# Four-layer attention kernel: weights' maxima from ScalarE magnitudes, half-precision parts on ScalarE, one chunk's queries moved into the first tail

## The chip, the cores and the metric

The kernel runs on one core of a Trainium2 chip. Its engines each have an instruction queue of their own that is served in order: TensorE (PE in the profile; its weight loads are PEld), VectorE (DVE), ScalarE (ACT), GpSimd (POOL) and SyncE (SP), which issues the transfers. The metric is the device time of one execution in microseconds, as the median of several runs. Before the change it is 2862.91 us (three runs, 2860.83 to 2866.21).

## The reference

Four layers, A, B, A, B, each adds its attention to the stream x (2048 tokens of 512). A is attention over a sliding window of 256 tokens, B over all tokens; both have 32 heads of 16. A layer normalises its input over the features, without weights.

```python
x = A_x
x = x + _A_ref(_layernorm(x, axis=-1), A_wqkv, A_wo)
x = x + _B_ref(_layernorm(x, axis=-1), B_wqkv, B_wo)
x = x + _A_ref(_layernorm(x, axis=-1), A_wqkv, A_wo)
x = x + _B_ref(_layernorm(x, axis=-1), B_wqkv, B_wo)

# both: q, k, v = x @ wqkv, split into 32 heads of 16
scores = jnp.einsum("bhqd,bhkd->bhqk", q, k) * (Dh ** -0.5)
scores = jnp.where(mask[None, None], scores, -1e9)   # A only: 0 <= i - j < 256
p = _softmax(scores, axis=-1)
o = jnp.einsum("bhqk,bhkd->bhqd", p, v)
return o.transpose(0, 2, 1, 3).reshape(B, S, D) @ wo
```

B_x is an input that nothing reads.

## The kernel before

**Tiling.** Tokens go in four chunks of 512 (NQ, index c), heads in four tiles of eight (NHT, index t) and eight quads of four (qd). A number that must be nearly of float32 precision is held as two float16 parts, a high part and the rest, and a projection takes three products of parts (TERMS). Twelve products of 128x128 by 512 (four slices of the features by three terms) make one tile of a projection, and four tiles one work of 48 products: K (keys), Q (queries), VV (values), OO (output projection with the next layer's normalisation).

**Preparing the weights.** Both layer types have four matrices: s = 0 queries, 1 keys, 2 values, 3 output. Each is scaled by a power of two per output column before it is split. `maxima` (line 277) finds the largest magnitude of each column: two VectorE reductions over the four slices, then transposes on TensorE and one more reduction. `scales` (line 305) makes powers of two and spreads them with a TensorE product. `parts` (line 327) multiplies by the scale, casts to the high part, subtracts for the low part and stores both (`wd`). Three matrices of A are prepared at the start by other functions (`first_maxima`, and `parts` with `act` true: VectorE multiplies, ScalarE casts). The other five go through `prep` (line 343) during layer 0, where GpSimd does all of `parts`: (0, 3) and (1, 1) in chunk 0, (1, 0) and (1, 2) in chunk 1, (1, 3) in chunk 2.

**Normalising.** `norm` (line 431) turns four tiles of tokens into `xn` (float32), its float16 high part `xh[:, 0]` and the rest `xh[:, 1]`, all on VectorE. A transposing transfer on SP's queue (T, line 461) then makes `xc`, from which K, Q and VV work.

**Attention.** Scores (line 663) go to PSUM, ScalarE takes their exponential `e` (line 667), in windowed layers GpSimd masks the edges of `e` (lines 729 and 732), and TensorE multiplies with the values (line 739 windowed, 707 full), two tiles of scores later. In layers 0 and 2 this alternates on TensorE with one tile of a work at a time. In layers 1 and 3 (`PH["full"]`) a work's products are cut into four strips of 32 columns (line 408) and spread over the steps.

**Order.** TensorE's order is that in which the program is written out: `attention` (line 897) runs the attention steps and draws works from lists (`side0` to `side3`, lines 1039 to 1071) by a clock of its own. A generator that yields a wait is taken up again when that clock has passed it. A tail, `tails[l]` (line 1075), holds the works between two layers; in it the first work that is ready goes first. `Side` with its due cost (line 808) spreads the works over the steps. The other engines' order, and the order of transfers on SP, come from the framework's scheduler. Two buffers hold weights (WB), four hold raw and prepared weights (tag `vf`).

Of the kernel before, what the change touches and what calls it, by code (L numbers as in the profile page):

```python
# [19 lines left out]
P = 128  # L20
# [168 lines left out]
def fast_path(ctx, tc, flag, a_x, a_wqkv, a_wo, b_wqkv, b_wo, out):  # L189
# [87 lines left out]
    def maxima(ty, s, raw):  # L277

        n = f"{ty}_{s}"
        if s == 3:  # L280
            for k in range(NC):
                nc.vector.tensor_scalar(raw[:, k, :], raw[:, k, :], upv[:, ty, k:k + 1], None, op0=ALU.mult)
        cm = CM[ty, s] = vp.tile([P, NHT], F32, name=f"wc{n}", tag="wc", bufs=8)
        am = vp.tile([P, D], F32, name=f"wa{n}", tag="dn", bufs=2)
        for h in range(2):
            f = slice(h * D // 2, (h + 1) * D // 2)
            nc.vector.tensor_reduce(am[:, f], raw[:, :, f].rearrange("p k f -> p f k"), axis=AX.X, op=ALU.max,
                                    apply_absolute_value=True)
            yield
        pt = bank().rearrange("p (t f) -> p t f", f=P)  # L290
        for t in range(NHT):
            nc.tensor.transpose(pt[:, t, :], am[:, t * P:(t + 1) * P], ident)
        nc.vector.tensor_reduce(cm, pt, axis=AX.X, op=ALU.max)
# [33 lines left out]
    def parts(ty, s, raw, act):  # L327

        dnb = DN.pop((ty, s))
        w = wp.tile([P, NC, 2, D], F16, name=f"w{ty}_{s}", tag="vf", bufs=NQ)  # L330
        for k in range(NC):
            r = raw[:, k, :]
            (nc.vector if act else nc.gpsimd).tensor_tensor(r, r, dnb, ALU.mult)
            if act:
                nc.scalar.activation(w[:, k, 0, :], r, AF.Copy)
            else:
                nc.gpsimd.tensor_copy(w[:, k, 0, :], r)
            nc.gpsimd.tensor_tensor(w[:, k, 1, :], r, w[:, k, 0, :], ALU.subtract)  # L338
            yield
        nc.sync.dma_start(wd[ty, s], w)  # L340
        WT[ty, s] = w

    def prep(ty, s):
        raw = load_w(ty, s)
        yield wait(14)
        for _ in maxima(ty, s, raw):
            yield wait(4)
        yield -spent(1.0)
        for _ in scales(ty, s):
            yield wait(4)  # L350
        if (ty, s) == (1, 0):
            share(1)
        yield -spent(0.5)
        for _ in parts(ty, s, raw, False):
            yield wait(2.5)
        WT.pop((ty, s))

# [73 lines left out]
    def norm(l, c, xs):  # L431

        mv = ST.pop((l, c))[1]
        y = rsqrt(nc, vp, f"{l}_{c}", mv[:, :, 1])
        out = []
        for i in range(4):
            xn = vp.tile([P, D], F32, name=f"xn{l}_{c}_{i}", tag="xn", bufs=1)
            xh = vp.tile([P, 2, D], F16, name=f"xh{l}_{c}_{i}", tag="xh", bufs=XNB)
            norm1 = lambda o: nc.vector.tensor_scalar(o, xs[i], mv[:, i, 0:1], y[:, i:i + 1], op0=ALU.subtract, op1=ALU.mult)  # L439
            norm1(xn)  # L440
            norm1(xh[:, 0])
            nc.vector.tensor_tensor(xh[:, 1], xn, xh[:, 0], ALU.subtract)  # L442
            out.append(xh)
# [587 lines left out]
    def F(*parts):  # L1031

        def gen():
            for p in parts:
                fill(*p)
                yield wait(8)
# [20 lines left out]
    def side1():  # L1057
        a = [Q(1, c, False) for c in (1, 2, 3)]
        for c in range(3):
# [3 lines left out]
    def side3(t, c):  # L1063
# [5 lines left out]
        if (t, c) != (0, 0):  # L1069
# [4 lines left out]
             [side3(t, c) for t in range(NHT) for c in range(NQ)]]  # L1074
    tails = {0: [OO(0, 3), VV(1, 2), T(1, 3), K(1, 3)],
             2: [OO(2, 3), VV(3, 1), VV(3, 2), Q3(0, 0, True), T(3, 3), K3(3, 0, True)]}
# [49 lines left out]
```

## Time and profile before

The profiled execution took 2864.46 us; its span, from the first to the last instruction, is 2862.7 us.

| | before |
|---|---|
| median of three runs | 2862.91 us |
| lowest, highest | 2860.83, 2866.21 us |
| profiled execution, its span | 2864.46 us, 2862.7 us |
| busy in the span: PE, ACT, DVE, POOL | 2668.1 (93%), 2352.5 (82%), 1048.1 (37%), 627.5 (22%) us |
| mean granted TensorE clock | 0.979 |
| transfers | 363.10 MB, 127 GB/s |

How to read it: the page cuts the span into 40 equal slices and gives the busy share of each in tenths. A table by windows has one row a stretch, with start and end in us, its length, busy us of each engine with the number of instructions in brackets, the granted clock as a share of full speed, the transfers' share and GB/s. A list of waits has who waited on which line, for whom, and total us, number and longest. A group has line, engine, operation, output and inputs by the program's names, shapes and count; then busy us, mean ns of one; then the idle time before them and what ended it. A timeline row has start, duration, engine, line and operation; the bracket at its end is the engine's idle time before it and what ended that. SPq is SP issuing transfers. The clock of a stage and its waits are read together.

### The profile page before, as it was taken

The page shows a single profiled execution, that of the slowest core. Times are in us where ns is not written, and L with a number is a line of the kernel's source. Part 1 is how long each engine was busy: PE and PEld are TensorE (multiplying, and loading weights), DVE is VectorE, ACT ScalarE, POOL GpSimd, SP SyncE. Part 2 cuts the span into 40 slices and gives each one's busy share as a digit, 9 for nine tenths or more (in the row PEclk, how much of TensorE's full clock was granted, in tenths as well). Part 3 has the DMA queues.
Part 4 walks back from the last instruction along what each step waited for, and adds up shares of the span by engine and source line. Part 5 has one row for each costly group of instructions (what it writes and reads, how often), then busy time and mean ns, then how long its engine had stood idle before and what let it go on. Part 6 is the DMA issues. An engine that isn't in the chain of part 4 may idle for free.

```text
span 2862.7 us, 58733 instructions
## 1 busy us (share of the span) xinstructions
PE 2668.1 (93%) x23298; PEld 766.6 (27%) x23298; DVE 1048.1 (37%) x2194; ACT 2352.5 (82%) x2643; POOL 627.5 (22%) x1183
## 2 busy tenths in 40 slices
PE   8777989799999999999999888999999999999997
PEld 4222433322222222222223333322222222222221
DVE  7667656411113212311224667722222322223222
ACT  3443656299999999999996666569999999999996
POOL 3547565101100000000003567500000000000000
PEclk9888999899999999999999999999999999999998
DMA  6857666522223222322343665542433333333331
GB/s 225 229 181 191 219 189 201 179 101 88 88 70 104 90 70 88 111 83 70 97 112 116 177 189 146 161 135 89 126 102 103 113 121 119 111 101 110 112 97 57
DMA packets 317423, 363.10 MB, mean 127 GB/s; under 512 B 120913, under 2 KB 223825, under 8 KB 309841
## 3 DMA queue, kind: packets, MB, share of 16 engines
q1 hardware_dynamic: 317136, 359.24, 41.5%
q8 instruction: 185, 3.03, 0.4%
q14 instruction: 102, 0.83, 0.1%
HBM read 229.64 MB, written 96.99 MB: 114 GB/s over the span
## 4 chain that ended last, share of the span: by engine, by line
PE 68%; ACT 10%; DVE 8%; issue 6%; DMA 3%; POOL 3%; SPq 1%; ACTq 0%; DVEq 0%; POOLq 0%
PE acc L707 28%; PE s L663 18%; ACT e L667 9%; PE b L411 9%; PE acc L408 8%; PE acc L739 3%; PE bs L411 2%; DVE ot L633 1%; DMA oh<-hl 1%; DVE xh L442 1%; SPq L650 1%; POOL w L338 1%; POOL e L732 1%; DVE xn L439 1%; DVE xh L439 1%
## 5 line engine op out<-in xcount | busy, mean ns | idle before, releaser
L667 ACT ACTIVATE e<-s 128x1024 f32<-128x1024 f32 (+2 forms) x2432 | 2235.3, 1199 | 115.1 <-PE s L663 108.1
L707 PE MATMUL acc<-e,vt 128*17 128x512 f32 x8192 | 1078.0, 598 | 3.7 <-DVE ot L633 1.5
L663 PE MATMUL s<-qt,kt 64*128 64x512 f16 (+3 forms) x5504 | 791.1, 355 | 70.8 <-ACT e L667 36.3
L663 PEld LDWEIGHTS <-kt 64*128 64x128 f16 x5504 | 222.6, 94 | 894.6 <-issue 851.3
L646 POOL TENSOR_TENSOR hl<-o,hl 128x512 f16<-128x512 f32 x64 | 74.2, 1159 | 999.8 <-DVE hl L645 923.3
L633 DVE STREAM_TRANSPOSE ot<-acc 128x512 f32<-128x512 f32 x128 | 91.2, 712 | 545.6 <-PE acc L707 448.0
L732 POOL TENSOR_SCALAR_AFFINE_SELECT e<-e 128x256 f32<-128x256 f32 x512 | 229.6, 456 | 160.1 <-ACT e L667 159.7
L739 PE MATMUL acc<-e,vt 128*17 128x384 f32 (+2 forms) x2816 | 213.4, 398 | 27.5 <-POOL e L729 26.6
L729 POOL TENSOR_SCALAR_AFFINE_SELECT e<-e 128x256 f32<-128x256 f32 x448 | 205.3, 464 | 113.7 <-ACT e L667 111.8
L707 PEld LDWEIGHTS acc<-e,vt 128*17 128x17 f32 x8192 | 136.3, 95 | 343.6 <-issue 314.5
L411 PE MATMUL b<-xc,w 128*128 128x512 f16 x636 | 154.6, 396 | 7.3 <-DMA xc<-xh 6.2
L492 DVE TENSOR_SCALAR sp<-acc,es 128x512 f16<-128x512 f32 x32 | 23.9, 748 | 323.6 <-PE acc L408 323.6
L490 ACT ACTIVATE sp<-b,es 128x512 f16<-128x512 f32 x53 | 36.4, 687 | 123.4 <-PE b L411 119.5
L498 POOL TENSOR_TENSOR sq_h<-sp_h 128x512 bf16<-128x512 f16 x27 | 29.1, 1077 | 451.5 <-DVE sp_h L492 451.5
L408 PE MATMUL acc<-xc,w 128*32 128x512 f16 x1536 | 127.2, 379 | 0.4 <-DVE sp L493 0.2
L498 POOL TENSOR_TENSOR sq<-sp 128x512 bf16<-128x512 f16 x32 | 33.3, 1039 | 405.3 <-DVE sp L492 405.3
L411 PE MATMUL b<-wv,xc 128*128 128x512 f16 x456 | 110.1, 395 | 11.0 <-DMA wv<-wd 11.0
L408 PE MATMUL acc<-xc,w_h 128*32 128x512 f16 x1296 | 114.5, 379 | 2.3 <-DVE km L530 2.3
L586 ACT ACTIVATE vt<-b 128x512 f32<-128x512 f32 x38 | 22.7, 597 | 102.7 <-PE b L411 102.7
L621 DVE TENSOR_TENSOR dx<-acc,gcol 128x512 f32<-128x512 f32 x60 | 41.5, 691 | 178.8 <-PE acc L408 178.8
L408 PE MATMUL acc<-wo,oh 128*32 128x512 f16 x1296 | 102.8, 379 | 0.7 <-DVE m L542 0.7
L411 PE MATMUL b<-wo,oh 128*128 128x512 f16 x390 | 91.5, 384 | 9.7 <-DMA oh<-hl 9.0
(164 smaller groups left out, 1728.0 us busy)
## 6 DMA issues: line engine op xcount, KB each, us to landing
kt<-kf SPq DMA_DIRECT2D x128, 512.0 KB
qt<-qs SPq DMA_DIRECT2D x128, 256.0 KB
xd<-x SPq DMA_DIRECT2D x96, 256.0 KB
x<-xd SPq DMA_DIRECT2D x96, 256.0 KB
w<-wd SPq DMA_DIRECT2D x22, 1024.0 KB
kt<-kw SPq DMA_DIRECT2D x64, 256.0 KB
oh<-hl SPq DMA_DIRECT2D x512, 32.0 KB
wv<-wd SPq DMA_DIRECT2D x15, 1024.0 KB
```

The costliest lines, as they stand in the source:

```text
L408: nc.tensor.matmul(ps[g:g + 32], a[:, g:g + 32], b, start=(i == 0), stop=(i == len(pairs) - 1), skip_group_check=True)
L411: nc.tensor.matmul(ps, a, b, start=(i == 0), stop=(i == len(pairs) - 1))
L439: norm1 = lambda o: nc.vector.tensor_scalar(o, xs[i], mv[:, i, 0:1], y[:, i:i + 1], op0=ALU.subtract, op1=ALU.mult)
L498: nc.gpsimd.tensor_tensor(sq, sp[:, 0], sp[:, 0], ALU.mult)
L633: nc.vector.transpose(ot.rearrange("p b r -> p (b r)"), a)
L646: (nc.gpsimd if l % 2 else nc.vector).tensor_tensor(hl[:, 1], o, hl[:, 0], ALU.subtract)
L663: nc.tensor.matmul(ps[:, h, s0:s0 + wd_], kt[R * h:R * h + R, pr, kc:kc + P], qt[R * h:R * h + R, pr, qc:qc + wd_], start=True, stop=True)
L667: nc.scalar.activation(e[:, :, w0:w1], ps[:, :, w0:w1], AF.Exp, scale=SCALE)
L707: nc.tensor.matmul(a[32 * h:32 * h + DH + 1, :], V[l, j // 4][:, j % 4, 4 * qd + h, :], es_[h // 2][:, h % 2, :], start=(j == 0), stop=(j ...
L729: nc.gpsimd.affine_select(v, v, pattern=[[0, 2], [-1, P]], compare_op=ALU.is_gt, fill=0.0, base=0, channel_multiplier=1)
L732: nc.gpsimd.affine_select(v, v, pattern=[[0, 2], [1, P]], compare_op=ALU.is_ge, fill=0.0, base=0, channel_multiplier=-1)
L739: nc.tensor.matmul(a[32 * h:32 * h + DH + 1, q * P:(q + nb) * P], V[l, (4 * c + j) // 4][:, j % 4, 4 * qd + h, :], es_[h // 2][:, h % 2, s ...
```

## The change

`maxima` now takes a prepared-weight tile at once and uses its high half, as bfloat16, for magnitudes that ScalarE writes slice by slice. VectorE takes three maxima of two slices each instead of the two reductions. The scaling of the output weights by `upv` moves from VectorE to ScalarE. `maxima` yields three times instead of two, and `prep` waits 3 instead of 4 at each.

`parts` runs its three steps shifted by one slice each, and the cast is ScalarE's always; GpSimd keeps the multiplication (where `act` is false) and the subtraction.

`norm` has ScalarE write the high part, as y times x plus nb, with nb = -mean times y a new 128x4 VectorE product. For l = 2 VectorE copies it from `xn` instead.

`F`, which writes constant rows of the score operands, waits 15 on the program's clock before its first fill. The queries of layer 1's chunk 1 move from `side1` to the first tail.

```diff
     def maxima(ty, s, raw):
         n = f"{ty}_{s}"
-        if s == 3:
-            for k in range(NC):
-                nc.vector.tensor_scalar(raw[:, k, :], raw[:, k, :], upv[:, ty, k:k + 1], None, op0=ALU.mult)
+        w = WT[ty, s] = wp.tile([P, NC, 2, D], F16, name=f"w{n}", tag="vf", bufs=NQ)
+        ab = w[:, :, 0, :].bitcast(BF16)
+        for k in range(NC):
+            if s == 3:
+                nc.scalar.activation(raw[:, k, :], raw[:, k, :], AF.Copy, scale=upv[:, ty, k:k + 1])
+            nc.scalar.activation(ab[:, k, :], raw[:, k, :], AF.Abs)
+            if k % 2:
+                yield
         cm = CM[ty, s] = vp.tile([P, NHT], F32, name=f"wc{n}", tag="wc", bufs=8)
         am = vp.tile([P, D], F32, name=f"wa{n}", tag="dn", bufs=2)
-        for h in range(2):
-            f = slice(h * D // 2, (h + 1) * D // 2)
-            nc.vector.tensor_reduce(am[:, f], raw[:, :, f].rearrange("p k f -> p f k"), axis=AX.X, op=ALU.max,
-                                    apply_absolute_value=True)
-            yield
+        for k in (0, 2):
+            nc.vector.tensor_tensor(ab[:, k, :], ab[:, k, :], ab[:, k + 1, :], ALU.max)
+        nc.vector.tensor_tensor(am, ab[:, 0, :], ab[:, 2, :], ALU.max)
+        yield
...
     def parts(ty, s, raw, act):
         dnb = DN.pop((ty, s))
-        w = wp.tile([P, NC, 2, D], F16, name=f"w{ty}_{s}", tag="vf", bufs=NQ)
-        for k in range(NC):
-            r = raw[:, k, :]
-            (nc.vector if act else nc.gpsimd).tensor_tensor(r, r, dnb, ALU.mult)
-            if act:
-                nc.scalar.activation(w[:, k, 0, :], r, AF.Copy)
-            else:
-                nc.gpsimd.tensor_copy(w[:, k, 0, :], r)
-            nc.gpsimd.tensor_tensor(w[:, k, 1, :], r, w[:, k, 0, :], ALU.subtract)
+        w = WT.pop((ty, s), None) or wp.tile([P, NC, 2, D], F16, name=f"w{ty}_{s}", tag="vf", bufs=NQ)
+        for k in range(NC + 2):
+            if k < NC:
+                (nc.vector if act else nc.gpsimd).tensor_tensor(raw[:, k, :], raw[:, k, :], dnb, ALU.mult)
+            if 0 < k <= NC:
+                nc.scalar.activation(w[:, k - 1, 0, :], raw[:, k - 1, :], AF.Copy)
+            if k > 1:
+                nc.gpsimd.tensor_tensor(w[:, k - 2, 1, :], raw[:, k - 2, :], w[:, k - 2, 0, :], ALU.subtract)
             yield
         nc.sync.dma_start(wd[ty, s], w)
-        WT[ty, s] = w
...
         for _ in maxima(ty, s, raw):
-            yield wait(4)
+            yield wait(3)
...
+        nb = vp.tile([P, 4], F32, name=f"nb{l}_{c}", tag="lnb")
+        nc.vector.scalar_tensor_tensor(nb, mv[:, :, 0], -1.0, y, op0=ALU.mult, op1=ALU.mult)
         for i in range(4):
...
-            norm1 = lambda o: nc.vector.tensor_scalar(o, xs[i], mv[:, i, 0:1], y[:, i:i + 1], op0=ALU.subtract, op1=ALU.mult)
-            norm1(xn)
-            norm1(xh[:, 0])
+            nc.vector.tensor_scalar(xn, xs[i], mv[:, i, 0:1], y[:, i:i + 1], op0=ALU.subtract, op1=ALU.mult)
+            if l == 2:
+                nc.vector.tensor_copy(xh[:, 0], xn)
+            else:
+                nc.scalar.activation(xh[:, 0], xs[i], AF.Identity, bias=nb[:, i:i + 1], scale=y[:, i:i + 1])
             nc.vector.tensor_tensor(xh[:, 1], xn, xh[:, 0], ALU.subtract)
...
     def F(*parts):
         def gen():
+            yield wait(15)
             for p in parts:
...
     def side1():
-        a = [Q(1, c, False) for c in (1, 2, 3)]
+        a = [Q(1, c, False) for c in (2, 3)]
...
-    tails = {0: [OO(0, 3), VV(1, 2), T(1, 3), K(1, 3)],
+    tails = {0: [OO(0, 3), VV(1, 2), Q(1, 1), T(1, 3), K(1, 3)],
```

On TensorE the order of the works stays as it was up to the first tail. There the moved queries come between the values of chunk 2 and the output projection of chunk 3. The transposes for the maxima and the products that spread the scales come one group later than before.

More of the change, by code (lines that the diff above doesn't have):

```diff
@@ L355, in prep @@
             yield wait(2.5)
-        WT.pop((ty, s))
     def share(ty):
```

## The prediction

> **What bounds the kernel now.** I read the page's 40 slices first. TensorE (PE) is full nearly everywhere but in the first fifth; ScalarE (ACT) is full in the two long plateaus and half empty before and between them.
>
> ```profile
> PE   8777989799999999999999888999999999999997
> ACT  3443656299999999999996666569999999999996
> ```
>
> Then the busy time by stage: layer 0 with its preparation is 0 to 520, its tail 520 to 580, layer 1 580 to 1520.
>
> ```profile
> core 0: us, PE busy (x) PEld busy (x) DVE busy (x) ACT busy (x) POOL busy (x), PEclk, DMA share, GB/s
> 100.00:200.00 100.00, 72.66 (x533) 26.14 (x533) 61.61 (x140) 46.08 (x65) 61.49 (x116) 0.90 0.67 195
> 200.00:300.00 100.00, 76.57 (x580) 29.89 (x580) 71.49 (x122) 40.41 (x49) 62.92 (x110) 0.84 0.67 188
> 520.00:580.00 60.00, 43.46 (x196) 18.51 (x193) 24.84 (x54) 9.45 (x15) 0.00 (x0) 0.86 0.52 167
> 580.00:1520.00 940.00, 928.36 (x8681) 219.81 (x8684) 203.12 (x452) 938.16 (x1018) 69.86 (x65) 1.00 0.29 88
> ```
>
> So layer 1 hangs on ScalarE (938.16 of 940.00). In layer 0 no engine is full, yet TensorE idles a quarter of the time: its order is written by hand, so it stands wherever the next product's input is late. Third, its waits from 0 to 580, as total, count, longest:
>
> ```profile
> PE acc L739 <- POOL e L729: 24.7, 10, 6.3
> PE bs L411 <- DMA xc<-xh: 15.4, 1, 15.4
> PE b L411 <- DMA wv<-wd: 11.0, 2, 8.2
> PE b L515 <- DVE sp L493: 8.4, 1, 8.4
> PE b L411 <- DMA xc<-xh: 6.2, 1, 6.2
> PE b L292 <- DVE km L530: 4.6, 1, 4.6
> ```
>
> The longest total is for GpSimd (POOL): its edge masks stand behind weight products and casts. The next is the gap in the tail, then a weight load late on SP's queue, then VectorE (DVE) twice. The change touches all of these, but only in layer 0 and the tails can it gain.
>
> **The change, part by part.** Groups up to 540 us:
>
> ```profile
> L338 POOL TENSOR_TENSOR w<-wr,w 128x512 f16<-128x512 f32 x32 | 41.6, 1316 | 48.3 <-ACT w L335 48.2
> L287 DVE TENSOR_REDUCE wa<-wr 128x256 f32<-128x1024 f32 x10 | 19.4, 1962 | 0.0
> L442 DVE TENSOR_TENSOR xh<-xn,xh 128x512 f16<-128x512 f32 x24 | 18.1, 753 | 0.1
> L439 DVE TENSOR_SCALAR xh<-x,mv,y 128x512 f16<-128x512 f32 x24 | 14.3, 617 | 0.0
> L337 POOL CAST w<-wr 128x512 f16<-128x512 f32 x20 | 13.6, 692 | 0.0
> L335 ACT ACTIVATE w<-wr 128x512 f16<-128x512 f32 x12 | 7.4, 630 | 11.9 <-DVE wr L333 11.9
> ```
>
> *Casts leave GpSimd.* Five prepared weights have four casts each: 20 x 0.692 = 13.8 us, 8 of them with each of two pairs of weights and 4 with the last. GpSimd's waits at TensorE add up to 24.7, more than 13.8, and come where the masks are queued behind this work, so I take all 13.8 as gain. Bounds: 24.7 if the waits go entirely, and nothing, if the masks are as late as before. On ScalarE the same casts cost 20 x 0.630 = 12.6 us, hidden in its empty half of layer 0 (row 200 to 300: 40.41 of 100); without that cover they would cost 12.6.
>
> *Maxima.* Per weight, two reductions of 1.962 us give way to four ScalarE magnitudes and three VectorE maxima, neither shown before. For a magnitude I take 0.630, the cast's row, between 0.6 and 0.7. For a maximum of two 512-wide rows I take 0.753, the row L442, the dearer end; half of it is the cheap one. The four scalings of each output weight move to ScalarE too and lie in the same cover. TensorE feels all this only at the two waits for VectorE:
>
> ```profile
> 199.38 0.62 PE L515 MATMUL b<-sq,hsum 128*32 128x512 bf16 x4 [8.44 <-DVE sp L493]
> 207.44 1.97 PE L292 MATMUL b<-ident,wa 128*128 128x128 f32 x8 [4.63 <-DVE km L530]
> ```
>
> There four half reductions (7.8 us) and four xh conversions (4 x 0.617 = 2.5) leave VectorE and six maxima (4.5) come: 5.8 less. But the evacuation sp that ends the first wait now starts on ScalarE behind four conversions and four magnitudes (8 x 0.630 = 5.0) that themselves wait for VectorE's statistics. So I take 4.0 of the 13.0; bounds 0 and 13.0.
>
> *Normalised tokens.* xh leaves VectorE in layers 0, 1 and 3's normalisations (layer 2's keeps it as a copy from xn, so ScalarE's plateau is not charged). It pays where the normalisation is waited for, in the tail:
>
> ```profile
> 518.77 2.76 PE L411 MATMUL bs<-wv,xc 128*128 128x512 f16 x12
> 526.55 2.75 PE L411 MATMUL b<-wv,xc 128*128 128x512 f16 x12
> 546.58 1.29 SPq L461 DMA_TRANSPOSE xc<-xh  x1
> 549.13 0.69 DVE L442 TENSOR_TENSOR xh<-xn,xh 128x512 f16<-128x512 f32 x1
> 550.44 0.69 DVE L442 TENSOR_TENSOR xh<-xn,xh 128x512 f16<-128x512 f32 x1
> 555.10 4.62 PE L411 MATMUL bs<-xc,w 128*128 128x512 f16 x12 [15.43 <-DMA xc<-xh]
> ```
>
> The last two tiles take 1.31 each with xh already done; four at that pace after the added 128x4 product instead of twelve operations bring the last xh about 1.2 us forward: -1.2 here, -1.2 in the tail of layer 2. Bounds 0 and 2.5 (four conversions).
>
> *Queries of chunk 1 in the first tail.* 48 products. Three groups of twelve start 7.78 us apart (518.77 to 526.55), 2.59 each: 4 x 2.59 = +10.4 us of a stage where TensorE is the bound. In the changed order they stand ahead of the output projection of chunk 3, and the gap of 15.43 us comes after that projection, so nothing fills it; its evacuations and twelve stores go under the projection. What layer 1 gets back: its first chunk, where these products stood, counted by exponentials (L667) and side products (L408):
>
> ```profile
> 640.00:700.00 60.00, 60.00 (x67) 1.00 0.30 95
> 760.00:820.00 60.00, 60.00 (x67) 1.00 0.26 81
> ```
>
> ```profile
> 640.00:700.00 60.00, 14.47 (x172) 4.87 (x164) 1.00 0.30 95
> 760.00:820.00 60.00, 6.26 (x72) 2.09 (x72) 1.00 0.26 81
> ```
>
> 67 exponentials in 60 us with 172 side products, and 67 with 72: ScalarE sets the pace, so taking products out gives nothing (bounds 0 and 10.4). The other eleven works of the layer need chunk 0's result and cannot move up.
>
> *SP's queue.* The scheduler reorders it. Early, one more transpose stands behind the fourth weight's load; late, the value weights of chunk 2 come ahead of two weight stores and two output moves:
>
> ```profile
> 71.53 8.81 SPq L461 DMA_TRANSPOSE xc<-xh  x2
> 252.63 3.98 PE L411 MATMUL b<-xc,w 128*128 128x512 f16 x12
> 267.91 0.58 SPq L376 DMA_DIRECT2D wv<-wd  x1
> 273.69 6.68 PE L411 MATMUL b<-wv,xc 128*128 128x512 f16 x18 [8.24 <-DMA wv<-wd]
> ```
>
> A transpose there costs 4.4 (8.81 / 2), in the tail 1.29; TensorE waits for it (6.2 above), so +3.0, between 1.3 and 4.4. The value load needs the slot that the products at 252.63 free, at 256.6, and could go 11 us before 267.91: the 8.24 falls away. But the next query tile's load stands behind it; I charge 3.0 for that: -5.2, bounds -8.2 and 0. Later starts of the constant fills touch no wait. The maxima's transposes and the scales' products move one group later in TensorE's order; they are the same instructions, and I charge nothing.
>
> *Cold products.* After the waits twelve products take 3.98 instead of 2.75, and eighteen 6.68 instead of 4.1 (1.5 x 2.75); one more such group:
>
> ```profile
> 132.02 2.19 PE L739 MATMUL acc<-e,vt 128*17 128x384 f32 x8 [6.32 <-POOL e L729]
> 136.89 3.83 PE L411 MATMUL b<-wv,xc 128*128 128x512 f16 x12
> 145.75 2.97 PE L739 MATMUL acc<-e,vt 128*17 128x384 f32 x16 [4.71 <-POOL e L729]
> ```
>
> 1.2 + 2.6 + 1.1 = 4.9, taken whole; bounds 0 and 4.9.
>
> *A rule weighed.* VectorE and GpSimd slow each other:
>
> ```profile
> 244.37 1.18 DVE L48 TENSOR_TENSOR z<-y,v 128x4 f32<-128x4 f32 x1
> 542.72 0.16 DVE L48 TENSOR_TENSOR z<-y,v 128x4 f32<-128x4 f32 x1
> ```
>
> The same tiny product takes 1.18 while GpSimd works on weights and 0.16 in the tail, where GpSimd is idle. The Trainium skill ("SBUF — State Buffer", section "Who interferes with whom") says that a VectorE instruction with two SBUF inputs contends with a GpSimd one that reads SBUF, and that a reduction never does. By that rule the change swaps ten innocent reductions for fifteen maxima that block GpSimd; as an estimate, if all fell on weight products, 15 x 0.753 = 11 us of the 13.8 would be given back. By the row above, taking casts off GpSimd also frees VectorE; I let the two cancel.
>
> **The sum.** +10.4 - 1.2 - 1.2 + 3.0 - 13.8 - 4.0 - 5.2 - 4.9 = -16.9. The profiled execution took 2864.46 (span 2862.7), 1.5 above the median of 2862.91: 2864.5 - 16.9 = 2847.6, or 2846 on the median's scale.
>
> **Rivals.** *All waits go, or the moved queries are free.* The waits for GpSimd, VectorE and value weights vanish: -24.7 - 13.0 - 11.0 - 4.9, with +10.4 - 2.4 + 1.3, is -44: 2819; free queries alone: 2836. For it: each of these waits ends on an instruction that the change shortens or moves. Against: behind each stands the next instruction of the same queue, and, for the queries, ScalarE's 67 in 60. Chance 0.15, about 2830.
>
> *The waits only change their names.* Masks still stand behind eight products instead of twelve operations, casts wait for GpSimd and GpSimd for casts; half of the gains of 27.9 remain (14.0) against +10.4 + 3.0 - 2.4 = 11.0: about 2860, no change. Chance 0.13.
>
> *Slower: ScalarE's queue is blocked.* It is served in order. Exponentials now stand behind casts that wait for GpSimd's fourth product, five GpSimd operations of 1.316 or 6.6 us, in layer 0's three preparation stretches, and behind conversions that wait for VectorE in eleven normalisations of layers 0 and 2. TensorE needs the scores' banks back, so beyond the one group of products between two score tiles (2.75) it stands: 6.6 - 2.75 = 3.9 for each of five weights, some 19, and 4 x 0.630 - 0.617 = 1.9 for each of eleven normalisations, 21. It decides from 17 us of such blocks on; at 19 + 21 = 40, with the gains: 2846 + 40 = 2886; with three quarters, 2876. Against: ScalarE is half empty there. Chance 0.20.
>
> **How the numbers follow.** Forecast 0.52, its own range 2836 to 2856. Range 2822 to 2870: beyond the low end lies about half of the first rival, beyond the high end the worse half of the last. 0.2% (5.7 us) is what can be told from no change: faster 0.68 (forecast, first rival and a sliver of the second), same 0.11, slower 0.21.
>
> **What would show it.** Right: waits for GpSimd masks near 11 instead of 24.7; the wait at 273.69 gone; the tail from 520 on some 9 us longer, the gap near 14; 580 to 1520's stage unchanged in length; the two VectorE waits near 9 together. Wrong: score products in layer 0 waiting for ScalarE exponentials by many us, a wait for qt or kt beyond 3, or layer 1 shorter by more than 2.

## The result and the profile after

The changed kernel takes 2869.5 us (median of 20 runs, 2861.5 to 2874.1), the kernel before 2863.2 (20 runs on the same chip): ratio 1.0020, 95% interval 1.0013 to 1.0027. It was forecast to become 17 us faster; it became 6 slower. The profiled execution took 2871.14 with a span of 2869.4 at a clock of 0.977, so 6.7 more than the one before. Where they lie, from the starts of the stages' first tiles on TensorE (the first value tile of the tail, the first scores of the next layer):

| stage | before, us | after, us | difference | forecast |
|---|---|---|---|---|
| layer 0 with its preparation | 518.8 | 515.7 | -3.1 | -24.9 |
| first tail | 61.4 | 72.0 | +10.6 | +9.2 |
| layer 1 | 955.5 | 955.7 | +0.2 | 0 |
| layer 2, its tail, layer 3 | 1327.1 | 1326.0 | -1.0 | -1.2 |

So the forecast failed in layer 0 alone. The longest waits of TensorE from 0 to 580 in the kernel after, to be laid beside those before:

```profile
PE s L669 <- ACT e L673: 36.9, 33, 7.2
PE b L413 <- DMA xc<-xh: 21.1, 2, 15.6
PE bs L307 <- DMA wr<-in_A_wqkv_dram: 10.3, 1, 10.3
PE b L413 <- DMA wv<-wd: 7.8, 1, 7.8
PE s L669 <- DMA kt<-kw: 7.3, 2, 5.3
PE b L413 <- DMA wo<-wd: 5.9, 1, 5.9
PE b L521 <- DVE sp L499: 5.7, 2, 3.0
PE acc L745 <- POOL e L735: 1.2, 2, 0.6
```

The wait for GpSimd's masks fell from 24.7 to 1.2, those for VectorE and the value weights fell too. In their place TensorE waits 36.9 for exponentials (10.4 before, in the same list of the kernel before), 7.3 for key tiles (2.1) and 5.9 for output weights (0.7). Summed over the same list, cut at the end of layer 0, all its waits are 83.6 after and 83.9 before: the waits changed their names. Two of the prediction's signs of being wrong are there, the exponentials and a wait for key tiles beyond 3. The gap in the tail is 15.6, not near 14. What ScalarE itself waited for from 60 to 515, by the list of its waits; the casts and conversions have such rows since the change:

```profile
...
ACT w L340 <- POOL wr L338: 23.3, 16, 3.7
ACT xh L447 <- DVE nb L439: 15.3, 5, 6.3
```

One such place in the timeline of ScalarE and then of TensorE (start, duration; in brackets the idle time before and what ended it):

```profile
138.50 0.63 ACT L340 ACTIVATE w<-wr 128x512 f16<-128x512 f32 x1 [3.32 <-POOL wr L338]
139.72 0.63 ACT L340 ACTIVATE w<-wr 128x512 f16<-128x512 f32 x1 [0.60 <-POOL wr L338]
140.95 0.63 ACT L340 ACTIVATE w<-wr 128x512 f16<-128x512 f32 x1 [0.59 <-POOL wr L338]
143.28 0.63 ACT L340 ACTIVATE w<-wr 128x512 f16<-128x512 f32 x1 [1.70 <-POOL wr L338]
143.81 1.49 ACT L673 ACTIVATE e<-s 128x768 f32<-128x768 f32 x2
...
136.52 4.22 PE L413 MATMUL b<-wv,xc 128*128 128x512 f16 x12
144.66 0.40 PE L669 MATMUL s<-qt,kt 64*128 64x256 f16 x2 [3.92 <-ACT e L673]
```

Four casts wait for GpSimd's products, two exponentials stand behind them, and TensorE stands 3.92 for the bank that they free. That is what the last rival of the prediction described. Whether it also cost the time is the question of the experiments.

### The profile page after: what moved, and what is told of

Same layout as the page of the kernel before. It is cut to its first block, busy times and chain, and to the rows that moved or that the text cites. A ratio compares the mean times of both kernels' runs of the same rounds, so it can differ in the third digit from the quotient of the medians.

```text
span 2869.4 us, 58527 instructions
## 1 busy us (share of the span) xinstructions
PE 2670.1 (93%) x23154; PEld 768.7 (27%) x23154; DVE 1002.9 (35%) x2158; ACT 2414.0 (84%) x2743; POOL 603.8 (21%) x1159
## 4 chain that ended last, share of the span: by engine, by line
PE 67%; ACT 14%; issue 7%; DVE 6%; DMA 3%; POOL 2%; SPq 1%; ACTq 0%; DVEq 0%; POOLq 0%
PE acc L713 26%; PE s L669 17%; ACT e L673 12%; PE b L413 10%; PE acc L410 8%; PE acc L745 3%; PE bs L413 2%; DVE ot L639 1%; ACT xh L447 1%; DMA w<-wd 1%; POOL e L738 1%; POOL e L735 0%; SPq L656 0%; DMA kt<-kw 0%; SPq L467 0%
## 5 line engine op out<-in xcount | busy, mean ns | idle before, releaser
L669 PE MATMUL s<-qt,kt 64*128 64x512 f16 (+3 forms) x5504 | 803.9, 358 | 114.3 <-ACT e L673 73.3
L738 POOL TENSOR_SCALAR_AFFINE_SELECT e<-e 128x256 f32<-128x256 f32 x512 | 228.8, 454 | 156.2 <-ACT e L673 155.6
L735 POOL TENSOR_SCALAR_AFFINE_SELECT e<-e 128x256 f32<-128x256 f32 x448 | 199.5, 451 | 141.5 <-ACT e L673 140.1
L745 PE MATMUL acc<-e,vt 128*17 128x384 f32 (+2 forms) x2816 | 206.6, 408 | 1.2 <-POOL e L735 1.2
L413 PE MATMUL b<-xc,w 128*128 128x512 f16 x672 | 160.5, 391 | 21.4 <-DMA xc<-xh 21.1
L410 PE MATMUL acc<-xc,w 128*32 128x512 f16 x1344 | 111.4, 379 | 0.2
L496 ACT ACTIVATE sp<-b,es 128x512 f16<-128x512 f32 x56 | 38.3, 685 | 83.9 <-PE b L413 76.3
L413 PEld LDWEIGHTS <-w 128*128 128x128 f16 x720 | 68.1, 100 | 121.8 <-issue 45.3
```

Source lines behind the costliest of these rows:

```text
L410: nc.tensor.matmul(ps[g:g + 32], a[:, g:g + 32], b, start=(i == 0), stop=(i == len(pairs) - 1), skip_group_check=True)
L413: nc.tensor.matmul(ps, a, b, start=(i == 0), stop=(i == len(pairs) - 1))
L669: nc.tensor.matmul(ps[:, h, s0:s0 + wd_], kt[R * h:R * h + R, pr, kc:kc + P], qt[R * h:R * h + R, pr, qc:qc + wd_], start=True, stop=True)
L735: nc.gpsimd.affine_select(v, v, pattern=[[0, 2], [-1, P]], compare_op=ALU.is_gt, fill=0.0, base=0, channel_multiplier=1)
L738: nc.gpsimd.affine_select(v, v, pattern=[[0, 2], [1, P]], compare_op=ALU.is_ge, fill=0.0, base=0, channel_multiplier=-1)
L745: nc.tensor.matmul(a[32 * h:32 * h + DH + 1, q * P:(q + nb) * P], V[l, (4 * c + j) // 4][:, j % 4, 4 * qd + h, :], es_[h // 2][:, h % 2, s ...
```

## The experiments

Each ran five rounds beside the kernel before on its chip; a ratio is against that. "Layer 0" is the length of the stage above in the profiled execution. Two runs below (a2, b2) leave layer 0 as it was before and change the tail alone; with before itself they have 518.3, 518.8 and 519.9. The changed kernel and a1, which differ in the tail alone, have 515.7 and 513.7. So differences in layer 0 up to about 2 us are not read, and one of 3.5 is read with care.

The scheduler orders the transfers on SP anew for every kernel. Only a3, f1 and c3 keep, in layer 0, the order of transfers of the kernel that each is compared with; the other edits of layer 0 change that order too.

### The moved queries

Run a1 puts them back in the changed kernel; run a2 moves them alone in the kernel before.

```diff
-        a = [Q(1, c, False) for c in (2, 3)]
+        a = [Q(1, c, False) for c in (1, 2, 3)]
...
-    tails = {0: [OO(0, 3), VV(1, 2), Q(1, 1), T(1, 3), K(1, 3)],
+    tails = {0: [OO(0, 3), VV(1, 2), T(1, 3), K(1, 3)],
```

> The changed kernel with the queries of chunk 1 back among layer 1's side products. Theory (the queries cost the first tail 48 products of TensorE and layer 1, set by ScalarE, gives nothing back): the first tail goes from 72.0 us back to about 61.4, layer 1 stays within 1 us of 956, the time is 2869.5 - 10.6 = 2859, 0.9985 of before. Rival (the tail was longer for another reason, or layer 1 had got the products back): the time stays within 2 us of 2869.5.

> The kernel before with only the queries of chunk 1 moved into the first tail. Theory: the tail grows from 61.4 to about 71.8 us, nothing comes back, 2863.2 + 10.4 = 2873.6, 1.0036 of before. Rival (in the kernel before, where no other edit changes the order around them, the products are paid back by layer 1): within 2 us of 2863.

a1: 2857.9, ratio 0.9968 (0.9957 to 0.9978), layer 0 513.7, first tail 61.6. a2: 2874.9, ratio 1.0034 (1.0022 to 1.0046), first tail 73.2. Both as the theory had it: the queries cost 10.4 in the changed kernel (72.0 - 61.6) and 11.8 in the one before, and layer 1 gives nothing back. Without them the change is a gain.

Run b2 moves them in the kernel before too, but behind the output projection, into the gap of TensorE, by having them wait, in the program, for the transfer T(1, 3):

```diff
+        if (l, c) == (1, 1):
+            k = [("T", 1, 3)]
...
-        a = [Q(1, c, False) for c in (1, 2, 3)]
+        a = [Q(1, c, False) for c in (2, 3)]
...
```

> The kernel before with the queries of chunk 1 in the first tail, but behind the output projection of chunk 3, so that they fall into the gap in which TensorE waits 15.4 for the last transposed tokens. Theory (they cost only because they stand ahead of that projection): the tail stays near 61.4 to 63, the gap shrinks by 10.4 to about 5, 2863 to 2865. Rival (the evacuations of the queries delay the normalisation behind the projection, and the gap moves back with it): 2868 to 2874.

2870.3, ratio 1.0015 (1.0006 to 1.0024): by the time, between theory and rival. In TensorE's timeline the fourth query tile, which now stands behind the projection, and the first key tile after it:

```profile
548.84 2.75 PE L411 MATMUL bs<-xc,w 128*128 128x512 f16 x12
559.95 4.36 PE L411 MATMUL b<-xc,w 128*128 128x512 f16 x12 [8.36 <-DMA xc<-xh]
```

The gap is 8.36, not 5, and the tail 64.8, 3.5 over 61.4: the gap hides 7 of the 10.4, and VectorE's part of the queries' evacuations (four of 0.75) stands among the normalisation's operations and delays them.

### The casts, the conversions and the maxima undone, and the maxima alone

Run a3: the casts of the five prepared weights on GpSimd again. Run a4: the first part of the normalised tokens on VectorE again. Run e2: the reductions again, in the version with the queries back. Run b1: the maxima's edit without the moved casts, conversions, queries and constant fills; the order of the three steps in `parts`, shifted by one slice each, stays as in the changed kernel, so b1 is not the maxima alone. The shift of `parts` and the later fills were undone by no run of their own.

```diff
@@ a3 @@
-                nc.scalar.activation(w[:, k - 1, 0, :], raw[:, k - 1, :], AF.Copy)
+                if act:
+                    nc.scalar.activation(w[:, k - 1, 0, :], raw[:, k - 1, :], AF.Copy)
+                else:
+                    nc.gpsimd.tensor_copy(w[:, k - 1, 0, :], raw[:, k - 1, :])
@@ a4 @@
-                nc.scalar.activation(xh[:, 0], xs[i], AF.Identity, bias=nb[:, i:i + 1], scale=y[:, i:i + 1])
+            nc.vector.tensor_scalar(xh[:, 0], xs[i], mv[:, i, 0:1], y[:, i:i + 1], op0=ALU.subtract, op1=ALU.mult)
@@ e2 @@
-            nc.scalar.activation(ab[:, k, :], raw[:, k, :], AF.Abs)
...
-            nc.vector.tensor_tensor(ab[:, k, :], ab[:, k, :], ab[:, k + 1, :], ALU.max)
...
+            nc.vector.tensor_reduce(am[:, f], raw[:, :, f].rearrange("p k f -> p f k"), axis=AX.X, op=ALU.max,
+                                    apply_absolute_value=True)
```

> The changed kernel with the casts of the five weights prepared in layer 0 on GpSimd again (same lag of the loop). Theory (ScalarE's queue stands at the casts that wait for GpSimd's products, and the exponentials behind them hold TensorE): ScalarE's waits of 23.3 and 16 us for GpSimd's products go, TensorE's waits for exponentials from 0 to 600 fall from 37.6 to 22 or less, its waits for GpSimd's masks come back to 12 to 25; these two nearly cancel, 2865 to 2873. Rival (the casts do not hold the exponentials up, only the conversions that wait for VectorE do): waits for exponentials stay above 32, masks come back, 2882 or more.

> The changed kernel with the first part of the normalised tokens on VectorE in every layer, as in the kernel before. Theory (ScalarE's queue stands at these conversions, which wait for VectorE's statistics): the stalls of TensorE at 252.97 (3.62) and 360.71 (7.20) go, the tail of layer 2 loses its 1.2 us again, about 2869.5 - 10.8 + 1.2 = 2860. Rival (the stalls only move to the next late input, since twelve operations of 0.617 more stand on VectorE ahead of the evacuations): 2867 to 2873.

> The changed kernel with the queries back in layer 1 and the maxima by VectorE's reductions (and the four scalings of an output weight on VectorE) as in the kernel before. Theory (the magnitudes and maxima took 5.8 us from VectorE ahead of the two waits for it, and gave 4.0 to TensorE): TensorE's waits for VectorE and the matching weight load come back by 4, layer 0 about 518, 2862. Rival (the two-input maxima hold GpSimd up and four ScalarE operations a weight hold the exponentials up, so the edit costs as much as it gives): layer 0 within 2 us of 513.7 or shorter, waits for exponentials under 33, 2854 to 2859.

> The maxima's edit alone (bfloat16 magnitudes on ScalarE, maxima and transposes as in the changed kernel); casts on GpSimd, first parts on VectorE, queries in layer 1. Theory (4.0 less at the two waits for VectorE, as predicted, nothing else moved): 2859 to 2861, layer 0 about 514 to 516. Rival (the maxima with two inputs hold GpSimd up where the reductions did not): the masks' waits rise above 24.7, layer 0 is 520 or longer, 2864 to 2874.

a3: 2872.8, ratio 1.0030 (1.0017 to 1.0042), layer 0 519.2. The waits for exponentials fell to 26.6 (the theory had 22 or less), those for masks came back to 15.2 (theory 12 to 25), and the time is in the theory's range: the casts' move is worth some 3.5 in layer 0, not 13.8. The ratio's interval overlaps that of the changed kernel, 1.0013 to 1.0027.

a4: 2882.4, ratio 1.0063 (1.0050 to 1.0075), layer 0 522.0, first tail 73.0. Theory and rival both fall: with the conversions back on VectorE layer 0 is 6.3 longer and the tail 1.0, though ScalarE stood 15.3 before them. The three longest waits of TensorE in layer 0 of a4:

```profile
PE s L664 <- ACT e L668: 22.2, 25, 5.7
PE s L664 <- DMA kt<-kw: 14.9, 3, 8.0
PE b L413 <- DMA wo<-wd: 10.2, 2, 7.3
```

14.7 less for exponentials (36.9 to 22.2), and 11.9 more for key tiles and output weights (7.3 + 5.9 to 14.9 + 10.2). Three waits of a4 have no counterpart in the changed kernel: 3.66 for weights at 281.56, 2.89 for output weights at 333.54 and 8.00 for key tiles at 375.78, together 14.6. The order of transfers is another one too: the second load of output weights is issued at 316.2 ahead of four moves of attention outputs in the changed kernel, and at 328.4 behind them in a4. So the 6.3 belongs to the conversions and to that order together.

e2: 2878.4, ratio 1.0053 (1.0039 to 1.0066), layer 0 535.1, 21.4 longer than a1's. b1: 2868.6, ratio 1.0018 (1.0008 to 1.0029), layer 0 522.3, 3.5 longer than before. So the maxima's edit, with the shifted `parts`, comes with 3.5 more by itself, and undoing it among the others costs 21.4; the theory (4 either way) fell twice. In e2 the rival fell as well. In b1 its signs came: masks waited for 27.7, more than 24.7, layer 0 above 520, the time in its range. But GpSimd's operations hardly became longer there (products 1.357 against 1.323, casts 0.687 against 0.692), so that the maxima hold GpSimd up is not shown. In e2 the waits for key tiles are 12.6, one of them 9.87 where a1 has none beyond 5.2, and VectorE waits 13.7 once for a tile of tokens: the order of transfers differs as well, and these runs do not take the two apart.

### ScalarE's waits taken away, its work left

Run c1 issues each cast two products later; run d2 puts the conversions of layer 1's normalisations, and what follows them, 5 us of the program's clock later in the order. Run f1 has the casts read the scale factor, which is long ready, instead of GpSimd's product, so its weights are not the layer's and only its time is of use. Run f2 takes the conversions with constants instead of the statistics. All on a1.

```diff
@@ c1; the differences likewise @@
-            if 0 < k <= NC:
-                nc.scalar.activation(w[:, k - 1, 0, :], raw[:, k - 1, :], AF.Copy)
+            if 2 < k <= NC + 2:
+                nc.scalar.activation(w[:, k - 3, 0, :], raw[:, k - 3, :], AF.Copy)
@@ d2, behind nb in norm @@
+        yield wait(5 if l == 1 else 0)
...
@@ f1 @@
-                nc.scalar.activation(w[:, k - 1, 0, :], raw[:, k - 1, :], AF.Copy)
+                nc.scalar.activation(w[:, k - 1, 0, :], raw[:, k - 1, :] if act else dnb, AF.Copy)
@@ f2 @@
-                nc.scalar.activation(xh[:, 0], xs[i], AF.Identity, bias=nb[:, i:i + 1], scale=y[:, i:i + 1])
+                nc.scalar.activation(xh[:, 0], xs[i], AF.Identity, bias=onesf[:, 1:2], scale=onesf[:, 0:1])
```

> The changed kernel with the queries back in layer 1 and each cast of a prepared weight issued two products later (cast of k after product k+3, difference after that), so that ScalarE finds its input ready. Theory (exponentials stand behind casts that wait for GpSimd): ScalarE's waits for GpSimd's products fall from 23.3 to under 8, TensorE's waits for exponentials from 38.3 to 25 or less, layer 0 from 513.7 to 505 or less, about 2849. Rival (the exponentials would be late anyway, since without the masks' wait ScalarE is the next late engine): waits for exponentials stay above 32, layer 0 within 2 us of 513.7.

> The changed kernel with the queries back in layer 1 and the conversions put some 5 us later, the products of the weights on GpSimd as in the changed kernel. Theory: the stalls behind conversions (3.62 and 7.37 at 251.08 and 358.45, 3.02 at 467.56) go and those behind casts (4.91 and 5.73) stay; waits for exponentials from 37.4 to 25 or less, layer 0 from 513.7 to 504 or less, about 2848. Rival (late normalisation shows at the next products): layer 0 stays above 511, 2855 to 2865.

> The changed kernel with the queries back in layer 1, in which the casts of the five weights prepared in layer 0 read the factor that scales the weight, long ready, not GpSimd's product; the difference takes up the rest, so only the split of those weights into two parts is changed. Order and length of the instructions stay the same. Theory (exponentials stand behind casts that wait for GpSimd): ScalarE's waits for GpSimd's products, 23.3, go; the stalls of 4.91 and 5.73 go and some of the wait for key tiles behind an evacuation; layer 0 from 513.7 to 504 or less, about 2848. Rival (the exponentials are late anyway): layer 0 within 3 us of 513.7, 2856 to 2861.

> The changed kernel with the queries back in layer 1, in which the first part of the normalised tokens in layers 0, 1 and 3 is taken with constants as scale and bias, not with the statistics (the difference takes up the rest; values change, work does not). Theory (exponentials stand behind conversions that wait for VectorE's inverse root): the stalls of 3.62, 7.37 and 3.02 go, waits for exponentials in layer 0 from 37.4 to 25 or less, layer 0 from 513.7 to 505 or less, about 2849. Rival (VectorE, late with the same statistics, delays the evacuations and differences behind them as well, and these hold TensorE instead): waits for exponentials fall, others rise by as much, layer 0 within 3 us of 513.7.

c1 (2863.1, ratio 0.9990, 0.9981 to 0.9999; layer 0 518.5) and d2 (2863.4, ratio 0.9998, 0.9989 to 1.0007; layer 0 519.5) tell little: their levers did not reach, and both change the order of TensorE's products and of the transfers. ScalarE still waited 18.4 and 22.9 for products, and in d2 12.0 for the normalisation.

f1 tells more, since TensorE's products and SP's transfers keep their order: 2853.5, ratio 0.9968 (0.9954 to 0.9981), the same ratio as a1's; layer 0 512.1 against 513.7. ScalarE's wait for GpSimd's products is gone, and TensorE's two longest waits in layer 0 are these:

```profile
PE s L669 <- ACT e L673: 23.5, 25, 8.4
PE acc L745 <- POOL e L735: 12.9, 5, 6.6
```

13.9 less for exponentials than a1's 37.4, and 11.6 more for masks than its 1.3; all waits together are 82.8 against 81.5. a1 stood 5.73 for an exponential at 235.27. f1 passes there, to stand for a mask soon after; TensorE's timeline, and then GpSimd's, which shows why:

```profile
242.62 1.04 PE L745 MATMUL acc<-e,vt 128*17 128x256 f32 x4 [6.60 <-POOL e L735]
...
237.62 1.26 POOL L338 TENSOR_TENSOR wr<-wr,wd 128x512 f32<-128x512 f32 x1
238.84 3.37 POOL L342 TENSOR_TENSOR w<-wr,w 128x512 f16<-128x512 f32 x3
242.16 0.40 POOL L735 TENSOR_SCALAR_AFFINE_SELECT e<-e 128x256 f32<-128x256 f32 x1
```

The mask needed at 242 stands behind products and differences on GpSimd. The casts' wait was the same lateness seen through ScalarE.

f2: ratio 0.9998 (0.9989 to 1.0007), layer 0 521.8, 8.1 longer than a1's: exponentials 20.7, but output weights 12.0 (4.7 in a1), key tiles 11.5 (7.5). The theory falls, but the rival (layer 0 within 3 of 513.7) is not met either. f2 has a4's order in the same place, with that load of output weights at 328.7 behind four moves that it precedes in a1 (313.8), and waits of 3.30, 2.65 and 4.77 at 282.02, 333.65 and 373.76 that a1 has not: 10.7 together. So what the blocked conversions cost stays open.

### GpSimd's weight work taken away

Run c3 puts the twenty products of the prepared weights on VectorE (on a1); g2 does that alone to the kernel before; g1 adds the twenty differences to c3.

```diff
@@ c3; g2 the same with r in the kernel before @@
-                (nc.vector if act else nc.gpsimd).tensor_tensor(raw[:, k, :], raw[:, k, :], dnb, ALU.mult)
+                nc.vector.tensor_tensor(raw[:, k, :], raw[:, k, :], dnb, ALU.mult)
@@ g1 @@
-                nc.gpsimd.tensor_tensor(w[:, k - 2, 1, :], raw[:, k - 2, :], w[:, k - 2, 0, :], ALU.subtract)
+                (nc.gpsimd if act else nc.vector).tensor_tensor(w[:, k - 2, 1, :], raw[:, k - 2, :], w[:, k - 2, 0, :], ALU.subtract)
```

> The changed kernel with the queries back in layer 1 and the twenty products of the prepared weights' scaling on VectorE, not GpSimd. Theory (the casts hold ScalarE because GpSimd's products of 1.316 are late): a product of about 0.75 on VectorE is ready sooner, ScalarE's wait for it falls from 23.3 to under 10, waits for exponentials to 25 or less, layer 0 505 or less, about 2849. Rival (fifteen us more on VectorE delay statistics, evacuations and keys): waits for VectorE and for the query and key tiles grow by 5 or more, layer 0 514 or longer, 2857 to 2868.

> The kernel before with one edit: the twenty products of the weights prepared in layer 0 on VectorE, not GpSimd. Theory (GpSimd's products hold the masks up in the kernel before as they held the casts up in the changed one): waits for masks from 24.7 to 10 or less, layer 0 from 518.8 to 508 or less, about 2853. Rival (in the kernel before VectorE still has the reductions and all conversions, so its waits of 8.4 and 4.6 grow by what the masks' fall): layer 0 within 4 us of 518.8, 2860 to 2868.

> The kernel with the twenty products on VectorE and the queries in layer 1, with the twenty differences of the same weights on VectorE too, so that GpSimd does only masks and constants there. Theory (GpSimd's weight work, and the sharing of memory with VectorE, sets the pace of the preparation): twenty operations of about 1.3 leave GpSimd, waits for its masks under 1, layer 0 from 505.3 to 500 or less, 2844 or less. Rival (VectorE is the next late engine, 20 x 0.69 = 14 us more on it): waits for VectorE and for the query and key tiles grow, layer 0 505 or longer, 2848 to 2858.

c3: 2847.5, ratio 0.9930 (0.9917 to 0.9944), layer 0 505.3, 8.4 less than a1; the exponentials' wait fell to 30.2 only, where the theory had 25 or less. g2: 2852.9, ratio 0.9967 (0.9955 to 0.9979), layer 0 508.9, 9.9 less than before (the theory had 508 or less, and 10 or less for the masks). Its four longest waits, from 0 to 580:

```profile
PE b L411 <- DMA wv<-wd: 16.7, 2, 12.1
PE bs L411 <- DMA xc<-xh: 15.6, 1, 15.6
PE acc L739 <- POOL e L729: 14.4, 9, 3.7
PE s L663 <- ACT e L667: 12.0, 23, 1.0
```

The masks' wait fell by 10.3 and 5.7 of it came back at the value weights (11.0 to 16.7), with VectorE's long wait unchanged (8.4). So moving products of 26.2 us off GpSimd is worth 8 to 10 in either kernel. Not all of that is waits: over layer 0 their sum falls by some 4 in g2 and 5 in c3, and the rest lies in TensorE's busy time for the same products (434.1 to 428.5, and 432.0 to 429.0). Nor is it GpSimd's queue alone. In g2 VectorE has twenty operations more in layer 0 and is busy as long as before (338.5 against 337.5 us), so its others became shorter, while on GpSimd a cast grew from 0.692 to 0.847 and a difference from 1.316 to 1.417. What the shorter queue and what the quicker VectorE is worth, these runs do not take apart.

g1: 2843.9, ratio 0.9937 (0.9923 to 0.9950), layer 0 503.7: 1.6 less than c3, which is not read as a difference. In c3 no cast waits for GpSimd and the masks' wait is 2.2, so little is left to get there. c3 and g1 beat both kernels.

Four more runs stand on c3: d1 and e1 put the conversions 5 and 14 us later in the order, as d2 did, f3 gives the conversions constants as f2 did, f4 puts them on VectorE as a4 did.

> The kernel with the twenty products on VectorE and the queries in layer 1, in which the conversions of the normalised tokens (and the operations behind them on VectorE) are put some 5 us later in the order, behind exponentials that follow (layer 1's normalisations alone). Theory (what is left of the waits for exponentials stands behind conversions that wait for VectorE's inverse root): the stalls at 244.24 (8.43), 349.66 (6.45) and 459.15 (2.89) go, waits for exponentials in layer 0 fall from 30.2 to 15 or less, layer 0 from 505.3 to 495 or less, about 2838. Rival (the normalisation is itself on the path, so that its delay shows at the next products as a wait for the transposed tokens): layer 0 stays above 503, waits for transposed tokens or query and key tiles grow by as much, 2846 to 2855.

> As the last run with products on VectorE, but the normalisations of layer 1's chunks 0 to 2 put some 14 us later in the order, so that the conversions stand one or more groups of exponentials behind the inverse root that they need. Theory (exponentials stand behind conversions): ScalarE's waits for the bias of the normalisation fall from 13.5 to under 5, waits for exponentials in layer 0 from 29 to 18 or less, layer 0 from 504.9 to 497 or less, about 2843. Rival (exponentials are the next late thing on ScalarE whatever stands ahead of them): ScalarE's waits for the bias fall, but TensorE's waits for exponentials stay above 25, layer 0 within 3 us of 505.

> The kernel with the twenty products on VectorE and the queries in layer 1, and besides the first part of the normalised tokens taken with constants (values change, work does not): neither kind of operation holds ScalarE up for long. Theory: both gains add, waits for exponentials in layer 0 at 18 or less, as little as the 10.4 of the kernel before plus the few us of more work on ScalarE, layer 0 496 or less, about 2840. Rival (the gains do not add, since behind each stall the next late input follows within a few us): layer 0 501 to 506, 2845 to 2850.

> The kernel with the twenty products on VectorE and the queries in layer 1, with the first part of the normalised tokens on VectorE too, as in the kernel before. Theory (what the conversions cost on ScalarE's queue they cost on VectorE's as well, as the run with them back there showed): layer 0 506 to 512 against 505.3, tails 1 us longer each, 2850 to 2858. Rival (without GpSimd's products on the shared memory VectorE has room for them and ScalarE's stalls of 8.43 and 6.45 go for nothing): layer 0 498 or less, 2842 or less.

Ratios 0.9959 (0.9945 to 0.9973), 0.9946 (0.9933 to 0.9960), 0.9974 (0.9963 to 0.9984) and 0.9980 (0.9970 to 0.9990); layer 0 504.9, 499.2, 511.5 and 512.7. None beats c3 in time. In f3 exponentials are waited for 16.7 in layer 0 instead of 30.2, and it is 6.2 longer, with output weights at 12.0 (6.0 in c3) and key tiles at 12.4 (7.6); in f3 and f4 the same load of output weights has moved as in f2 and a4, so this too is not the conversions alone. In d1 ScalarE still waited 13.5 for the normalisation, in e1 11.2, so the fall under 5 that the theory needed did not come; e1's shorter layer 0 comes with key tiles at 16.6 and did not show in the median (2848.8 against 2847.5). The profiled execution of c3, 2853.4, lies 5.9 above its median, that of e1 at its own.

## Why the prediction was wrong

**The step that failed** is "so I take all 13.8 as gain" for the casts that leave GpSimd, together with "hidden in its empty half" for their new place. Its sign was right, and the masks' wait fell even further than forecast, to 1.2. But the move is worth some 3.5 (a3), because the casts' own input, GpSimd's product, was late as well, and ScalarE serves its queue in order: the exponentials took over the masks' lateness. An empty half of an engine hides work only if the work's input is there when its turn comes. What both kernels share is the products on GpSimd, which the change left there: the step from a3 to the changed kernel turns masks' waits into exponentials', the step from a1 to f1 turns them back, each with the transfers in the same order, and c3 and g2, which take the products away, gain 8.4 and 9.9. The rest of the missing 21.8 (24.9 - 3.1) lies in the terms below and is only in part accounted for.

**Value weights, -5.2.** The wait at 273.69 went, but the later one grew from 2.8 to 7.8: -3.2 in all (11.0 to 7.8), within the bounds. What is late next was asked of the query tile only, not of the next load of value weights.

**VectorE, -4.0; cold products, -4.9; transposes on SP, +3.0.** The two waits of 13.0 became one of 2.7, and one of 3.0 is new at 106.24: 7.3 less. But TensorE then comes 11 us earlier to the first tile of the output projection, and its weights, 0.74 late before, are now 5.92 late (at 209.26): that takes 5.2 back, and 2.1 of the 4.0 remain. TensorE's busy time in layer 0 fell by 2.1 (434.1 to 432.0), not 4.9. The early wait for transposed tokens is 5.5 against 6.2: the 3.0 charged for the transposes did not come.

**Maxima.** The pieces were cheaper than assumed (a magnitude takes 0.62 against 0.630, two of three maxima 0.43 and the third 0.74 against 0.753); the edit's worth was not foreseen at all: it is -21.4 (e2) or +3.5 (b1) by what stands around it, other transfers' order included. The range of no term held that. Terms that share queues in layer 0 do not add: undone one at a time, casts, conversions and maxima come with 3.5, 6.3 and 21.4, together with the rest 3.1.

**Normalised tokens.** 0.630 was the row of a cast; the conversion takes 0.804 by the groups of the kernel after (the third row is GpSimd's product, used further down):

```profile
L447 ACT ACTIVATE xh<-x,nb,y 128x512 f16<-128x512 f32 x24 | 17.7, 804 | 16.7 <-DVE nb L439 16.7
L340 ACT ACTIVATE w<-wr 128x512 f16<-128x512 f32 x32 | 19.8, 629 | 34.5 <-POOL wr L338 23.3 <-DVE wr L338 11.1
...
L338 POOL TENSOR_TENSOR wr<-wr,wd 128x512 f32<-128x512 f32 x20 | 26.2, 1331 | 0.0
```

The difference is 0.175, and the conversion has two operands more, with one value per partition each. The Trainium skill ("ScalarE: Activation LUTs", section "What ACT_TABLE_LOAD costs") gives about 93 ns for each such operand, as an estimate 0.186 for two; the trace is near it. The tail of layer 2 gained the 1.2 that was forecast. In the first tail a4 shows 1.0, but with the queries back it is 61.6 against 61.4 before, so that gain did not show there.

**Queries, +10.4; layer 1, 0.** Right: 10.4 in the changed kernel, 11.8 alone, and 0.2 in layer 1; the first rival's free queries are out.

**The rivals.** "The waits only change their names" is what layer 0 did, and more so than priced: 3.1 of 24.9 remained, not half. "ScalarE's queue is blocked" had the place right and the price wrong: the long stalls behind casts and conversions add up to 23.5 (3.92, 5.71, 3.62, 7.20, 3.02), not 40, and f1, which takes those behind casts away, has the time of a1. For those behind conversions f2 does not settle it.

## What to carry to other kernels

In a stretch where no engine is full and one engine's order is fixed, the sum of that engine's waits is a stock: before counting a wait as gain, find the next input that is late at the same place, and the operation whose lateness both share; here taking that one off its engine paid (c3, g2), and freeing one of those that wait for it did not (f1). An edit that changes what waits for what can also change the order that a scheduler gives to the transfers; compare the orders before the times are read. Work moved to a half-empty engine brings its wait along, and what stands behind it in that queue waits too. Products that come ahead of a gap of their engine cost their full time (a1, a2), even when the gap follows at once.

## What the runs showed of the hardware

Small VectorE operations take longer while GpSimd works on weights. The inverse root of the same normalisation in the kernel after (with GpSimd on products and differences) and in c3 (with masks alone), four of its rows each, from VectorE's timeline, and first three of GpSimd's rows beside it in the kernel after:

```profile
238.75 1.16 POOL L342 TENSOR_TENSOR w<-wr,w 128x512 f16<-128x512 f32 x1
239.86 1.27 POOL L338 TENSOR_TENSOR wr<-wr,wd 128x512 f32<-128x512 f32 x1
241.09 2.27 POOL L342 TENSOR_TENSOR w<-wr,w 128x512 f16<-128x512 f32 x2
...
238.85 1.08 DVE L45 TENSOR_SCALAR y<-v 128x4 int32<-128x4 int32 x1
239.96 1.19 DVE L46 TENSOR_SCALAR y<-y 128x4 int32<-128x4 int32 x1
241.19 1.07 DVE L48 TENSOR_TENSOR z<-y,v 128x4 f32<-128x4 f32 x1
...
248.21 0.32 DVE L439 SCALAR_TENSOR_TENSOR nb<-mv,y 128x4 f32<-128x4 f32 x1
```

```profile
237.15 0.31 DVE L45 TENSOR_SCALAR y<-v 128x4 int32<-128x4 int32 x1
237.50 0.33 DVE L46 TENSOR_SCALAR y<-y 128x4 int32<-128x4 int32 x1
237.86 0.16 DVE L48 TENSOR_TENSOR z<-y,v 128x4 f32<-128x4 f32 x1
...
239.63 0.16 DVE L439 SCALAR_TENSOR_TENSOR nb<-mv,y 128x4 f32<-128x4 f32 x1
```

From the start of VectorE's first row to that of its last it takes 9.4 us in one and 2.5 in the other; the conversions on ScalarE wait for the last. The Trainium skill ("SBUF — State Buffer", section "Who interferes with whom") says that whoever issues first on the shared ports blocks the other for the whole instruction, for VectorE operations with two inputs, and for copies, casts and `tensor_scalar` in a two-port mode; the rows agree as to the length, each slow operation lasting about as long as one of GpSimd's (1.16 and 1.27). Two of the slow ones, the `tensor_scalar` rows at 238.85 and 239.96, have one input; whether they ran in that mode no row shows. What that rule made of the maxima in the prediction, 11 us given back by GpSimd, was not seen: its products take 1.331 in the kernel after (the group's row above) and 1.323 before. In g2, where the twenty products of two inputs stand on VectorE, GpSimd's casts take 0.847 instead of 0.692.
